# Filter rotation straight from float32, a cosine table made by a matmul, a fourth spectrum buffer and a new order table

## The chip, the cores and the metric

The kernel runs on one core of one Trainium2 chip. Its engines are TensorE (PE for matmuls, PEld for loading their stationary operands), VectorE (DVE), ScalarE (ACT), GpSimd (POOL) and SyncE (SP), which here issues every DMA. The metric is the device time of one execution in microseconds (us); less is better. Three runs of the kernel before gave 462.65, 462.97 and 460.04; their median is 462.65.

## What is computed

`x` and `f_logit` are 4 x 6272 x 256 (batch, time, channel), float32. The first half is a gated recurrence over time, the second a long convolution of its output, done in the frequency domain and gated on both sides:

```python
    f = lower_bound + (1 - lower_bound) * sigmoid(f_logit); i = 1 - f
    for t in range(S):                       # S = 6272
        h = f[:, t] * h + i[:, t] * x[:, t]; y[:, t] = h
    proj = y @ w_proj                        # 256 -> 3 * 256
    x1, x2, x3 = split(proj)
    conv = irfft(rfft(x2, axis=time) * rfft(filter_fft, axis=time))
    out = (x1 * conv * x3) @ w_out
```

## The kernel before

The length 6272 is 49 x 128, so each transform is done in two steps by matmuls with small tables of sines and cosines, kept in `D1`, `FT`, `VA`, `VB` and `ID` (in float16) and, for the filter, `D1r` and `FTr`. Work on one batch `b` goes through these steps, named as the planner names them:

- `hgrn(b)`: 13 chunks of 512 time steps. Each loads a piece of `f_logit` and of `x` (512 KB each, `load`, into three slots of `FL` and `XT`, for batch 0 also into `XS`), takes a sigmoid (`sig`, ScalarE, L334), a product (`u`, GpSimd, L336), and for each half of the channels transposes both (`su`, TensorE, L348), scales the gate (`f`, ScalarE L361 or VectorE L363) and runs the recurrence (`scan`, VectorE, L369) into `HA`. `wrap` copies the start of each sequence behind its end, on GpSimd, ScalarE or as a DMA of SP.
- `phase_p(b)` (`P`, L713) projects x2 and `x2` copies it into `X2`; `phase_f1`, `mini` and `unit` (`F1` L726, `F2` L785, `I2` L825) transform 16 units of 8 channel pairs forward and back. Between `F2` and `I2` each half unit is multiplied by the filter's spectrum: straight from PSUM on VectorE (L806), or copied by ScalarE or VectorE and multiplied on GpSimd (`pm`, L815). A unit's spectrum is loaded from DRAM into one of NH = 3 buffers `Hu` (`H`, L763); the order of use reverses from batch to batch, so that the buffers' contents serve twice at a turn.
- `gate(b)` (`x13`, L397, then `xs`, `z`) projects x1 and x3 and multiplies them into `zt`.
- `phase_o(b)`: 13 groups of four rows (the last has one). `I1` (L865) ends the back transform, `y` (VectorE, L871) applies the gate, `proj` (L883) multiplies by w_out, `o` copies out of PSUM, `store` sends 512 KB to `out`. Staging buffers are three `osb` tiles (`NO`) and, for groups 3 to 6, borrowed room in `PP` and in the `A` part of `HA`.

`prepare` runs once, ahead of and beside `hgrn(0)`. It makes an identity (`iden`), rounds it to float32r as `rot`, computes the arguments of all tables on VectorE (`args0` for 520 columns, `args1` for 512 more, which only `ID` needs), takes sines of both on ScalarE (L559) and fills the tables. It scales w_proj and copies w_out on ScalarE (seven `W` operations). The filter comes in 13 loads (`ff`) into ten buffers, seven in `X2`, two in `Hu`, one in `HA`. A group is first rounded to float32r by a copy (`fr`) into `afs`, then each of its rows is rotated by a matmul with a window of `rot` (`rot`, L629), which shifts its partitions; two copies (`f2`) bring it to the layout of the first filter step. When all thirteen groups are there, `FF1` (L654), `afs`, `FF2` (L672) and `hw` make the filter's spectrum and `hst` (L681) stores it to DRAM. Twenty-four fillers (`warm`, L599, four float16 matmuls each) may be put anywhere on TensorE.

The order is not that of the code. `Plan.op` records every operation with its reads, writes and engines; the string `ORDER` then lists, in the order in which they are emitted, each operation's number, engine and PSUM bank. Each engine runs its own in that order, and SP issues its DMAs in that order, so an operation that waits holds up what stands behind it on its engine. The planner that made the string is not part of the kernel.

## Time and profile before

| | us |
|---|---|
| median of three runs | 462.65 |
| profiled execution, its own time | 464.51 |
| its span in the profile | 462.3 |
| TensorE busy / idle in the span | 440.1 / 22.2 |
| first matmul of FF1 | 23.0 |
| first matmul of P, batch 0 | in 60 to 80 |

The page names an instruction by line, engine, operation, output and inputs, shape and count; then come busy time and mean duration, and the engine's idle time just ahead of it with what ended most of that. Views by time give start and length in us. Views by stage give busy time of each engine, the clock that TensorE was granted (1.00 is full) and the mean busy share of the core's 16 DMA engines. Rows of the page that the prediction does not use:

```profile
PEclk9799999999999999999999999999999899999999
DMA  8999999857987995668959983787969822655176
...
L336 POOL TENSOR_TENSOR XT<-XT,FL 128x1024 f32<-128x1024 f32 (+1 forms) x49 | 109.8, 2243 | 60.3 <-ACT FL L334 40.9
L369 DVE TENSOR_TENSOR_SCAN HA<-fTs,HA,PS 128x512 f16<-128x512 f32 (+1 forms) x96 | 112.5, 1202 | 6.3 <-ACT fTs L361 5.5
L815 POOL TENSOR_TENSOR PP<-HA,Hu 98x1008 f16<-98x1008 f16 x52 | 109.2, 2107 | 10.0 <-ACT HA L283 8.6
L397 PE MATMUL PS<-HA,W 128*128 128x490 f16 (+1 forms) x416 | 101.5, 367 | 0.8 <-DVE HA L369 0.5
```

The first two lines cut the span into 40 slices, in tenths: TensorE's granted clock and the DMA engines' busy share.

### The profile page before, as it was taken

To read this page: it belongs to the slowest core of one execution; us is meant where nothing else is said; L and a number is where in the kernel's file an instruction comes from. 1 tells how busy PE (TensorE), PEld (TensorE's weight loads), DVE (VectorE), ACT (ScalarE), POOL (GpSimd) and SP (SyncE) were. 2 spreads that over 40 slices of the span, in tenths; PEclk is the share of its full clock that TensorE was granted. 3 is DMA by queue.
4 is the path that set the end of the run, shared out by engine and by line. 5 is a ranking of instruction groups with operands and counts; after the bars stand their busy time and mean duration, and the time that the engine had idled before them with its cause. 6 is when DMAs were issued, how large, how long until landed. Compare 5 with 4: busy or idle time off the path is not lost.

```text
span 462.3 us, 14627 instructions
## 1 busy us (share of the span) xinstructions
PE 440.1 (95%) x6009; PEld 347.8 (75%) x6009; DVE 408.1 (88%) x475; ACT 403.6 (87%) x577; POOL 310.3 (67%) x283
## 2 busy tenths in 40 slices
PE   7799889999999999999999999999999899999998
PEld 5677668767767889777668898676768797767787
DVE  8889988799999994899999987999999847999963
ACT  5899898899999989999998988999999778988462
POOL 6978795476999634978997526889986303876400
PEclk9799999999999999999999999999999899999999
DMA  8999999857987995668959983787969822655176
GB/s 323 408 349 336 357 316 339 306 155 214 342 293 253 342 358 181 227 193 272 338 212 331 363 276 145 229 298 262 333 214 300 309 92 84 196 181 183 59 304 255
DMA packets 44530, 121.66 MB, mean 263 GB/s; under 512 B 4272, under 2 KB 6960, under 8 KB 44464
## 3 DMA queue, kind: packets, MB, share of 16 engines
q1 hardware_dynamic: 44464, 120.73, 74.8%
q8 instruction: 47, 0.77, 0.7%
q14 instruction: 19, 0.16, 0.1%
HBM read 87.69 MB, written 31.98 MB: 259 GB/s over the span
## 4 chain that ended last, share of the span: by engine, by line
PE 64%; DVE 11%; ACT 9%; DMA 6%; POOL 5%; issue 4%; SPq 1%; DVEq 0%; POOLq 0%; ACTq 0%
PE PS L397 16%; PE PS L825 8%; PE PS L883 7%; PE PS L713 7%; PE PS L348 7%; PE PS L785 6%; PE PS L726 6%; DVE HA L369 5%; DMA FL<-in_f_logit_dram 3%; PE PS L865 3%; DVE ys L871 3%; POOL XT L336 2%; POOL PP L815 2%; ACT FL L334 2%; ACT fTs L361 1%
## 5 line engine op out<-in xcount | busy, mean ns | idle before, releaser
L336 POOL TENSOR_TENSOR XT<-XT,FL 128x1024 f32<-128x1024 f32 (+1 forms) x49 | 109.8, 2243 | 60.3 <-ACT FL L334 40.9
L369 DVE TENSOR_TENSOR_SCAN HA<-fTs,HA,PS 128x512 f16<-128x512 f32 (+1 forms) x96 | 112.5, 1202 | 6.3 <-ACT fTs L361 5.5
L815 POOL TENSOR_TENSOR PP<-HA,Hu 98x1008 f16<-98x1008 f16 x52 | 109.2, 2107 | 10.0 <-ACT HA L283 8.6
L397 PE MATMUL PS<-HA,W 128*128 128x490 f16 (+1 forms) x416 | 101.5, 367 | 0.8 <-DVE HA L369 0.5
L806 DVE TENSOR_TENSOR PP<-PS,Hu 98x1008 f16<-98x1008 f32 x76 | 89.9, 1200 | 4.2 <-PE PS L785 2.0
L283 ACT CAST HA<-PS 128x1024 f16<-128x1024 f32 (+1 forms) x104 | 83.0, 828 | 3.4 <-PE PS L785 1.5
L871 DVE TENSOR_TENSOR ys<-PS,zt 128x1024 fp32r<-128x1024 f32 (+1 forms) x52 | 58.3, 1151 | 10.6 <-PE PS L865 7.8
L361 ACT ACTIVATE fTs<-PS,nomc 128x512 f32<-128x512 f32 (+1 forms) x93 | 60.3, 669 | 3.0 <-PE PS L348 2.0
L883 PE MATMUL PS<-Wo,ys 128*128 128x256 f32 x392 | 58.5, 296 | 1.2 <-DVE X L288 0.6
L825 PEld LDWEIGHTS <-PP 98*128 98x128 f16 x1024 | 49.5, 98 | 12.4 <-POOL PP L790 2.6
L397 PEld LDWEIGHTS <-W 128*128 128x128 f16 x416 | 35.1, 97 | 29.6 <-issue 5.0
L285 ACT ACTIVATE XS<-PS 128x490 f32<-128x490 f32 (+1 forms) x90 | 51.6, 585 | 6.5 <-PE PS L397 4.3
L283 ACT CAST Th<-PS 128x784 f16<-128x784 f32 x61 | 50.1, 822 | 5.8 <-PE PS L825 4.8
L883 PEld LDWEIGHTS PS<-Wo,ys 128*128 128x128 f32 x392 | 50.5, 192 | 6.2 <-DVE ys L871 1.3
L334 ACT ACTIVATE FL<-FL 128x1024 f32<-128x1024 f32 (+1 forms) x49 | 49.3, 1012 | 6.7 <-DMA FL<-in_f_logit_dram 6.6
L418 DVE TENSOR_TENSOR zt<-PS,XS 128x490 f16<-128x490 f32 (+1 forms) x81 | 51.3, 649 | 3.4 <-PE PS L397 2.1
L825 PE MATMUL PS<-VA,PP 98*128 98x98 f16 x512 | 52.4, 207 | 1.3 <-POOL PP L790 0.8
L825 PE MATMUL PS<-VB,PP 98*128 98x98 f16 x512 | 52.1, 207 | 0.0
L427 POOL TENSOR_TENSOR zt<-XS 128x490 f16<-128x490 f32 x23 | 28.3, 1234 | 28.5 <-DVE ys L871 21.7
L713 PE MATMUL PS<-W,HA 128*128 128x256 f16 x392 | 44.1, 273 | 1.2 <-ACT X L283 0.6
L348 PE MATMUL PS<-iden,FL 64*128 64x64 f32 x736 | 41.9, 230 | 3.0 <-ACT PP L285 1.5
L713 PEld LDWEIGHTS <-HA 128*128 128x128 f16 x392 | 42.9, 142 | 2.1 <-issue 1.6
(117 smaller groups left out, 728.7 us busy)
## 6 DMA issues: line engine op xcount, KB each, us to landing
Hu<-H SPq DMA_DIRECT2D x55, 512.0 KB, 4.4
FL<-in_f_logit_dram SPq DMA_DIRECT2D x45, 512.0 KB, 6.1
XT<-in_x_dram SPq DMA_DIRECT2D x45, 512.0 KB, 6.5
out_dram<-osb SPq DMA_DIRECT2D x32, 512.0 KB, 4.1
X<-in_moe_filter_fft_dram SPq DMA_DIRECT2D x9, 512.0 KB, 7.6
out_dram<-PP SPq DMA_DIRECT2D x8, 512.0 KB, 6.1
out_dram<-HA SPq DMA_DIRECT2D x8, 512.0 KB, 4.4
H<-Hu SPq DMA_DIRECT2D x4, 512.0 KB, 7.5
```

The lines of the kernel that those rows point to most:

```text
L283: nc.scalar.copy(dst, src)
L336: op("u", {"POOL": 0.1 + 0.553 * nb}, lambda e, xt=xt, ft=ft: nc.gpsimd.tensor_tensor(xt, xt, ft, op=AOP.mult), r=[("ft", k)], w=[("xt", k)])
L348: nc.tensor.transpose(bank(pb)[:, at[p] + j:at[p] + hn:nb], src[ps, j, cols], iden[ps, ps])
L361: nc.scalar.activation(fT, sT, AF.Identity, scale=by, bias=1.0)
L369: nc.vector.tensor_tensor_scan(h, fT, bank(pb)[:, 512 - hn:512 + hn], init, op0=AOP.mult, op1=AOP.add),
L397: nc.tensor.matmul(PS[:, p, 0:n], W13[:, kh, js], HA[:, HB[kh] + t0:HB[kh] + t0 + n], start=(kh == 0), stop=(kh == 1))
L713: nc.tensor.matmul(pp[:, r - r0, :], column(HB[kh], q_of(r)), W2[:, kh, :], start=(kh == 0), stop=(kh == 1))
L806: nc.vector.tensor_tensor(pr, px.unsqueeze(1).broadcast_to([TB, 2, UE, 63]), hh, op=AOP.mult)
L815: nc.gpsimd.tensor_tensor(pr, spec[:, o, :, 1:64].unsqueeze(1).broadcast_to([TB, 2, UE, 63]), hh, op=AOP.mult)
L825: nc.tensor.matmul(PS[:, ib + o, pr * TB:(pr + 1) * TB], PP[:TB, k, o, n, 2 * pr:2 * pr + 2, :], v[:TB], start=(n == 0), stop=(n == 1))
L871: nc.vector.tensor_tensor(late["ys"][:, yk, :, 0:rn * 128], PS[:, cb:cb + 2, 0:rn * 128], late["zt"][:].rearrange("p k r m -> p k (r m)") ...
L883: nc.tensor.matmul(po[:, i, :], late["ys"][:, yk, kh, i * 128:(i + 1) * 128], Wo[:, kh, :], start=(kh == 0), stop=(kh == 1))
```

## The change

- Filter groups 0, 2, 4, 6, 8 and 10 (`WHOLE`) are no longer rounded: their rows are rotated straight from the loaded float32 data, with the same identity read as plain float32 (`rot4`, 24 matmuls). The seven others keep the `fr` copy.
- The arguments shrink from 1032 columns to 324: of each table only the sine and the cosine remain, and the others are made from these by sign. `args1` is gone; the sign columns become one operation (`signs`), which the order puts on GpSimd. `ID` is now made on TensorE by four matmuls of the first table with the identity (`flip`) and one ScalarE activation that scales by `wt` and repeats it (`flipped`).
- The seven `W` operations may run on GpSimd, and the order puts all seven there.
- The fillers go from 24 to 14; 6 instead of 11 of them stand in the front, 3 in the middle instead of 1, 3 among the last groups of outputs instead of 1, and 2 behind the last projection instead of 11.
- A fourth spectrum buffer (`Hl`) is made once the filter's scratch room is free: `NH` = 4, of which `NK` = 3 are in `Hu`. There are 52 loads `H` instead of 55.
- Two own staging buffers instead of three; `places` says where each output group is staged (`PP` is used for groups 2, 3, 8 and 9, the `A` part for 4 and 5). A place in `zt` is programmed and not used.
- `ORDER` is replaced as a whole. Between engines, over the whole kernel, it moves little: of `wrap` 26 instead of 32 are on GpSimd, 7 instead of 8 on ScalarE and 15 instead of 8 on SP; of the copies `A` 11 instead of 7 are on VectorE, of `xs` 19 instead of 15; the direct products on VectorE are 77 instead of 76.

```diff
-NH = 3
-NO = 3
-WARM = 24
+NH = 4
+NK = 3
+NO = 2
+WARM = 14
+WHOLE = (0, 2, 4, 6, 8, 10)
...
-            op("W", {"ACT": 0.6}, lambda e, kh=kh, by=by: act.activation(
+            op("W", {"ACT": 0.6, "POOL": 0.75}, lambda e, kh=kh, by=by: scaled(
...
-        small(iotas, 1260, r=["iden"], w=st + ["pint", "FT"], e="POOL", kind="iota")
+        small(iotas, 452, r=["iden"], w=st + ["pint", "FT"], e="POOL", kind="iota")
...
-            for i, k in enumerate((kre, kre, k2, k2)):
+            for i, k in enumerate((kre, k2)):
                 stt(w[:, 128 + 98 * i:226 + 98 * i], in0=cF, scalar=k,
-                    in1=oF[i], op0=AOP.mult, op1=AOP.add)
-            fold(0, 520)
-
-        def args1(e):
+                    in1=oF, op0=AOP.mult, op1=AOP.add)
+            fold(0, 324)
+
+        def signs(e):
...
-        def rest2(e):
+        def flip(e, p):
             for i in range(2):
-                pool.tensor_scalar(ID[:, i, :], in0=v[:, 520 + 256 * i:776 + 256 * i],
-                                   scalar1=wt, scalar2=None, op0=AOP.mult)
+                for h in range(2):
+                    nc.tensor.matmul(PS[64 * h:64 * h + 64, p, i * 128:i * 128 + 128],
+                                     v[:, i * 64:i * 64 + 64], iden[:], start=True, stop=True)
+
+        def table(e, p):
+            act.activation(ID[:].rearrange("p i (c j) -> p i c j", c=2),
+                           PS[:, p, 0:256].rearrange("p (i j) -> p i j", i=2).unsqueeze(2)
+                           .broadcast_to([128, 2, 2, 128]), AF.Copy, scale=wt)
...
-            op("fr", {"ACT": 0.08 + 0.214 * rn, "POOL": 0.1 + 0.235 * rn, "DVE": 0.1 + 0.267 * rn},
-               lambda e, raw=raw, fr=fr, rn=rn: copy(e, fr[:, 0:rn], raw[:, 0:rn]),
-               r=et, w=[("af", g % 2, 0), ("af", g % 2, 1)])
-            def rotate(e, pb, r0=r0, rn=rn, fr=fr):
+            whole = g in WHOLE
+            if not whole:
+                op("fr", {"ACT": 0.08 + 0.214 * rn, "POOL": 0.1 + 0.235 * rn, "DVE": 0.1 + 0.267 * rn},
+                   lambda e, raw=raw, fr=fr, rn=rn: copy(e, fr[:, 0:rn], raw[:, 0:rn]),
+                   r=et, w=[("af", k, 0), ("af", k, 1)])
+
+            def rotate(e, pb, r0=r0, rn=rn, fr=raw if whole else fr, rot=rot[:].bitcast(F32) if whole else rot):
                 pr = PS[:, pb:pb + 2].rearrange("m a (r e) -> m (a r) e", e=256)
                 for r in range(r0, r0 + rn):
                     nc.tensor.matmul(pr[:, r - r0, :], rot[:, m0_of(r):m0_of(r) + 128],
                                      fr[:, r - r0, :], start=True, stop=True)
-            rt = op("rot", {"PE": 0.12 * rn}, rotate, r=[("af", g % 2, 0), "rot"], take=2)
+            rt = op("rot4" if whole else "rot", {"PE": (0.43 if whole else 0.12) * rn}, rotate,
+                    r=(et if whole else [("af", k, 0)]) + ["rot"], take=2)
...
+    def hu(h):
+
+        return Hu[:, h] if h < NK else late["Hu"][:]
...
+    places = (("o", 0), ("o", 1), ("p", 0), ("p", 1), ("a", 0), ("a", 1), ("o", 0),
+                  ("o", 1), ("p", 0), ("p", 1), ("o", 0), ("o", 1), ("o", 0))
```

302 lines of the change are left out of this document (161 added, 141 removed).

## The prediction

> **What bounds the kernel now.** I read the page first (busy times, chain), then the busy time by stages, then the front (0 to 23 us) in order of time, then the stage behind it, and last the seams between batches and the tail.
>
> ```profile
> PE 440.1 (95%) x6009; PEld 347.8 (75%) x6009; DVE 408.1 (88%) x475; ACT 403.6 (87%) x577; POOL 310.3 (67%) x283
> ...
> PE 64%; DVE 11%; ACT 9%; DMA 6%; POOL 5%; issue 4%; SPq 1%; DVEq 0%; POOLq 0%; ACTq 0%
> ```
>
> TensorE is busy 440.1 of 462.3 us and carries 64% of the chain that ended last, so a saving on another engine counts only where it shortens TensorE's 22.2 us of idle time, or work that TensorE alone does. Where that idle time lies, the stages tell (start:end, length, then busy time of PE, PEld, DVE, ACT, POOL, granted clock, DMA share, GB/s):
>
> ```profile
> 0.00:23.00 23.00, 17.52 (x93) 13.63 (x94) 19.62 (x49) 16.42 (x26) 18.48 (x37) 0.85 0.94 365
> 23.00:60.00 37.00, 32.81 (x429) 26.17 (x430) 34.49 (x38) 34.47 (x50) 29.82 (x30) 1.00 0.98 350
> 60.00:100.00 40.00, 38.56 (x440) 30.46 (x437) 34.02 (x39) 35.77 (x52) 26.39 (x29) 1.00 0.82 280
> 100.00:300.00 200.00, 195.27 (x2878) 154.19 (x2875) 183.98 (x200) 186.62 (x266) 146.07 (x115) 1.00 0.78 267
> 300.00:400.00 100.00, 95.68 (x1408) 76.39 (x1408) 86.89 (x95) 90.51 (x133) 63.05 (x51) 0.98 0.69 236
> ```
>
> TensorE idles 5.5 us in the front, 4.2 in the next stage, 1.4 up to 100 us, then 4.7 in 200 and 4.3 in the next 100. The front is paced by DMA (share 0.94), and from 23 to 60 us VectorE and ScalarE are both 93% full (34.5 of 37): that stage, filter transform with the first recurrence, belongs to them.
>
> **The front: six casts out, 24 plain float32 matmuls in.** In order of time (start, length):
>
> ```profile
> 8.68 1.86 SPq L618 DMA_DIRECT2D X<-in_moe_filter_fft_dram  x3
> ...
> 23.00 2.92 PE L654 MATMUL PS<-D1r,f 128*128 128x256 f32 x20 [0.48 <-ACT f L283]
> ```
> ```profile
> X<-in_moe_filter_fft_dram SPq DMA_DIRECT2D x1, 128.0 KB, 9.3
> ```
> ```profile
> 1.64 5.95 DMA X<-in_moe_filter_fft_dram
> ...
> 8.67 1.28 ACT L559
> ...
> 12.27 0.60 PE PS L599 x4
> 12.87 0.63 PE PS L629 x4
> ...
> 20.19 1.23 PE PS L629 x4
> 21.45 1.73 ACT f L283 x4
> ```
>
> The third of the thirteen filter loads lands at 7.59 (1.64 + 5.95); the last is issued at about 10.2, as the end of three issues that finish at 10.54, and lands 9.3 later, at 19.5. Between the two lie 9.25 groups in 11.9 us: 1.28 each, so the second lands at 6.3 and the twelfth at 19.1. Behind the last come its rotation and evacuations; ScalarE's queue of evacuations ends at 23.18, and FF1 starts at 23.0. A group's four rotations take 0.63 at one time and 1.23 at another, which the granted clock explains (columns as above):
>
> ```profile
> 12.00:14.00 2.00, 1.21 (x8) 0.82 (x7) 2.00 (x2) 2.00 (x5) 1.94 (x2) 1.00 1.02 408
> 14.00:22.00 8.00, 7.33 (x30) 6.08 (x31) 6.55 (x11) 6.73 (x13) 7.60 (x12) 0.57 1.03 408
> ```
>
> A mean of 0.57 over 8 us, if the clock knows only full and half, is half for 6.9 of them; it fell after a stretch in which TensorE was busy 1.21 of 2 us.
>
> The change leaves the loads, so nothing before 19.5 can be won. What it does to the 3.5 us behind: the sine table load (1.28, at 8.67) leaves the middle of ScalarE's work, because the sine is now ScalarE's first instruction and its table loads while nothing has landed; two of its twenty evacuations go to VectorE, which no longer computes a second block of arguments. On TensorE a group straight from float32 costs an unknown; no plain float32 matmul of 256 columns is in the trace. Bounds by the nearest rows: below, the rounded rotation, 0.63 for four; above, the 512-column matmul of FF2:
>
> ```profile
> L672 PE MATMUL PS<-afs,FTr 64*128 64x512 f32 x64 | 11.0, 437 | 0.3 <-ACT afs L283 0.2
> ```
>
> 437 ns each, 1.75 for four. The nearest row in columns is the lower one, but its operands are the rounded ones that these groups give up; I take 1.75, since a lower price would win little more. Then six such groups and seven others (the last has one matmul) are 6 x 1.75 + 6 x 0.63 + 0.2 = 14.5 us, from the second landing on to 20.8. TensorE is nearly full, so that its clock should stay up, and it ends with the twelfth group (group 8): landed at 19.1, rotated by 20.9, the single matmul by 21.1, evacuated by 21.6. FF1 starts at about 21.7: 1.3 earlier. At 0.63 it would be 20.6, 2.4 earlier.
>
> The Trainium skill, FP8 and Floating Point Precision, section TensorE Precision Notes, says that true float32 makes four passes through the array; by that a group would cost an estimated 4 x 0.63 = 2.5, which I keep as a rival.
>
> New waits: the load of group 10 waits for the rotation of group 0, and that of group 12 for group 2's, the sixth on TensorE, ending at 6.3 + 4 x 1.75 + 2 x 0.63 = 14.6; on SP's queue behind it stand all loads of batch 0. The twelve groups ahead keep the DMA engines busy to 19.1, and a load takes some 4 us on an empty queue (the third's 5.95 less the 1.28 of each of two ahead, 3.4, is the nearest), so SP has about 1 us in hand: 0, but late from then on.
>
> The front's fillers go from 11 (four matmuls each, 0.60) to 6; nine of the eleven ran before the first rotation, so they cost and save nothing but the clock.
>
> **23 to 72 us.** The order tables say which engine does what between the last evacuation and the last scan of batch 0. ScalarE: seven W operations leave, copies of `afs` go from 18 to 22, of `hw` from 11 to 13, `f` from 19 to 17, one table activation enters. VectorE: `afs` 14 to 10, `hw` 3 to 2, `f` 7 to 9.
>
> ```profile
> L361 ACT ACTIVATE fTs<-PS,nomc 128x512 f32<-128x512 f32 x7 | 4.6, 686 | 0.4 <-PE PS L348 0.2
> L283 ACT CAST afs<-PS 128x512 fp32r<-128x512 f32 x8 | 4.6, 585 | 0.3 <-issue 0.3
> L285 ACT ACTIVATE Hu<-PS 128x1024 f16<-128x1024 f32 x4 | 4.1, 1016 | 0.0
> ...
> L476 ACT ACTIVATE W<-HA,omc 128x512 f16<-128x512 f32 x2 | 1.4, 750 | 0.0
> L481 ACT ACTIVATE W<-HA,omc 128x128 f16<-128x128 f32 x3 | 1.3, 438 | 0.0
> ```
> ```profile
> L288 DVE CAST afs<-PS 128x512 fp32r<-128x512 f32 x14 | 9.1, 678 | 1.0 <-issue 0.6 <-PE PS L672 0.4
> ```
>
> ScalarE: -2 x 0.75 - 4 x 0.44 for six W operations, about -0.6 for the seventh, +4 x 0.59, +2 x 1.02, -2 x 0.69, and some 0.7 for the table, a copy of 512 elements: about 0. VectorE: -4 x 0.68 = -2.7; its one spectrum copy less and two `f` more cancel, at ScalarE's prices to 0.4: -2.3. So the pair is 2.3 lighter, with one spectrum copy more done inside the stage, and the stage starts 1.3 earlier.
>
> GpSimd pays: it takes the seven W operations and the sign columns, and loses five casts, the ID table and two wraps.
>
> ```profile
> L589 POOL TENSOR_SCALAR ID<-PP,cols 128x256 f16<-128x256 f32 x2 | 1.8, 927 | 0.0
> ...
> L576 POOL TENSOR_SCALAR FT<-PP,cols 128x98 f16<-128x98 f32 x2 | 1.1, 576 | 0.0
> ```
>
> From 98 to 256 elements a scaling grows from 576 to 927 ns, 2.2 ns an element: 1.5 for each W13 half, 0.64 for each W2 piece, and by the same line 1.5 at most for Wo, a copy: 7.1 us at most, put around the third and fourth products of batch 0, with the recurrence behind them. The ID table (1.8) is gone, and the memset of X2's gaps, inside this stage before, now stands ahead of it: at most 5.3 net. GpSimd has 7.2 us of idle in 23 to 60, so this fits, if just; of TensorE's 4.2 idle there I count 1.5 as won (bounds: 2.5 won, 2.5 lost when GpSimd is late).
>
> **Seams and the rest.** The matmul work of the batches is the same, and switches between full and half-row work on TensorE are 208 before and 206 after, so no price. The largest seam stall, before batch 3:
>
> ```profile
> 353.67 8.79 DMA FL<-in_f_logit_dram
> ```
> ```profile
> 363.00:366.00 3.00, 1.38 (x40) 1.12 (x36) 1.85 (x2) 3.00 (x5) 2.36 (x1) 1.00 0.68 263
> 366.00:370.00 4.00, 3.97 (x37) 3.85 (x38) 4.00 (x4) 2.51 (x5) 0.74 (x1) 0.57 0.74 286
> ```
>
> A load lands 8.8 us after issue, because it stands behind two stores; ScalarE's evacuation stands behind the sigmoid of that load; TensorE idles 1.6 in 363 to 366, and then its clock is at 0.57 for 4 us, worth 1.7. In the new order loads 20 to 23 of batch 3 are issued ahead of store 1, so this landing comes two transfers earlier. I count 2.0 of the 3.3 as won; the rest I leave to new stalls of the same kind.
>
> Here the clock fell after 1.38 busy of 3 us, in the front after 1.21 of 2. The Trainium skill, TensorE: Matmul & The Clock Gate, section on HAM oscillation, asks for an idle gap above about 3.4 us; this trace disagrees: there was no room for one in either stretch.
>
> Fourth H buffer: 55 loads become 52; none of the sixty longest waits names a landed spectrum, so 0 either way. Seven more wraps go by SP: 7 x 0.6 less on GpSimd, not the bound there, 0. Output staging with two own buffers: the last group shares one with the group two before it, and four projections or fillers lie between, longer than a store's landing: 0. Fillers behind the front: before two ahead of the last projection, after six, 0.6 each; up to 2.4 if none is covered by a wait, I take 0.8 lost. The tail:
>
> ```profile
> 455.58 4.82 PE PS L599 x44
> ```
> ```profile
> 450.01 8.00 SPq L894 DMA_DIRECT2D out_dram<-osb  x6
> ```
> ```profile
> SPq L961 <- DMA out_dram<-osb: 3.1, 1, 3.1
> ```
>
> Eleven fillers run behind the last projection to 460.4, but SP, whose last store is issued by 458.0, waits 3.1 more for its landing, to 461.1: their removal saves nothing.
>
> **Sum.** The profiled run took 464.51 (span 462.3 and 2.2 around it). -1.3 - 1.5 - 2.0 + 0.8 = -4.0: 460.5. It stands 1.9 above the median 462.65; the same change from the median is 458.7. I take half a microsecond off the gain for stalls that a wholly new order opens: **459.2**.
>
> **Rivals.** (1) TensorE waits less everywhere: the 4.2 of the second stage go wholly and a third of the 10.4 behind it; 459.2 - 2.7 - (3.5 - 2.0) = 455.0. For it: VectorE lighter, a buffer more. Against: ScalarE no lighter there. (2) Idle time only moves: the front's gain is swallowed at the seams, as both copying engines stay full; 462. (3) GpSimd becomes the bound of the second stage: its 7.1 us of scalings delay the fourth product by 4.0 (less the 1.3 of the earlier start and the 1.8 taken away), of which the bound above lets 2.5 reach TensorE, instead of winning 1.5; 459.2 + 4.0 = 463.2. (4) Slower: the front becomes TensorE's. It decides if four float32 rotations take over 1.8, for then 6.3 + 6x + 4.0 is later than 19.1 + x + 0.2. At four times the rounded row, 2.5, rotation ends at 25.3 instead of 21.1: 463.4. If the clock falls as before as well, 6.9 us at half lose 3.4 more: 466.8. For it: TensorE has no slack at 1.75 already; against: a full TensorE is what kept the clock up in every other window. By the passes on the page named above and this row its first half would be certain. (5) Slower: the new order keeps the stall at 363 and makes another two like it: 459.2 + 2.0 + 6.6 = 467.8. (6) That the change does not do what it says: the sine's table could still load late; ScalarE's order excludes it, no chance.
>
> **Chances.** Forecast (457 to 462) 0.35; (1) 0.16; (2) 0.17; (3) 0.11; (4) 0.14; (5) 0.07. One per cent of 462.65, about what a measurement here can tell from no change, is 4.6: faster is under 458.0, slower over 467.3. Faster: (1) and 0.14 of the forecast, 0.30. Slower: 0.05 of (5) and 0.04 of (4), 0.09. Same: 0.61. The range goes from 454.5, under (1), to 466, near (4)'s end, and leaves out (5) and the rims.
>
> **What would show it.** Right: FF1's first matmul near 21.7; four float32 rotations near 1.75; clock 1.00 through 6 to 22; TensorE's idle in the second stage under 3; no wait over 1 us at the seam of batch 3. Wrong: rotations still running after 23, GpSimd without gaps from 24 to 50 with TensorE waiting on transposes, the clock at 0.5 in the front, or more than 11 us of TensorE idle behind 60.

## The result, and the profile after

The changed kernel took **458.62 us**, the median of 9 runs (456.89 to 460.24), beside 462.97 for the kernel before on the same chip (9 runs, 460.04 to 465.8): a ratio of 0.9922, 95% interval 0.9893 to 0.9951. The forecast was 459.2. A second set, run later, gave 457.84 beside 461.23, ratio 0.9925 (0.9902 to 0.9948). Its profiled run took 459.04, with a span of 457.2, where that of the kernel before had taken 464.51 and 462.3. The counts of runs and of clocks below leave out executions that were disturbed as a whole, three of e_nh3's six among them.

So the time came out as forecast; how it came about did not, in several steps. Busy times and the first line of the chain on the page of the changed kernel:

```profile
PE 438.0 (96%) x6001; PEld 347.9 (76%) x6001; DVE 402.7 (88%) x458; ACT 397.0 (87%) x564; POOL 304.7 (67%) x285
...
PE 67%; DVE 9%; ACT 9%; issue 6%; POOL 5%; DMA 3%; POOLq 0%; DVEq 0%; ACTq 0%; SPq 0%
```

TensorE has 2.1 us less work and 3 us less idle time (19.2 of 457.2, before 22.2 of 462.3). By stages (columns as in the prediction: start:end, length, busy time of PE, PEld, DVE, ACT, POOL, granted clock, DMA share, GB/s):

```profile
0.00:23.00 23.00, 20.05 (x105) 16.33 (x105) 12.18 (x30) 12.47 (x20) 16.91 (x46) 1.00 0.93 357
23.00:60.00 37.00, 34.05 (x440) 27.36 (x440) 33.45 (x37) 35.87 (x50) 33.71 (x34) 1.00 0.96 347
60.00:100.00 40.00, 38.04 (x446) 30.39 (x446) 33.65 (x38) 36.69 (x53) 18.75 (x20) 1.00 0.91 323
...
300.00:400.00 100.00, 98.23 (x1440) 77.99 (x1439) 92.60 (x103) 89.54 (x131) 68.17 (x57) 1.00 0.68 233
```

The clock stands at 1.00 where it was 0.85 and 0.98. TensorE's idle time in the second stage goes from 4.2 to 3.0 and in 300 to 400 from 4.3 to 1.8. But ScalarE and VectorE, 4.0 and 7.4 us lighter in the front than before, did not bring FF1 forward. The front's end, in order of time (start, length, engine, line, operation, and in brackets the idle time before it and what ended it):

```profile
17.72 1.89 PE L645 MATMUL PS<-X,rot 128*128 128x256 f32 x8
...
19.26 0.82 PE L645 MATMUL PS<-afs,rot 128*128 128x256 f32 x4
...
19.92 1.89 PE L645 MATMUL PS<-Hu,rot 128*128 128x256 f32 x8
...
21.56 0.37 PE L645 MATMUL PS<-afs,rot 128*128 128x256 f32 x1
21.86 0.66 PE L594 MATMUL PS<-iden,PP 128*64 128x128 f32 x8
...
21.92 0.69 DVE L294 CAST f<-PS 128x512 fp32r<-128x512 f32 x1 [0.51 <-PE PS L645]
...
22.64 0.91 ACT L289 CAST f<-PS 128x512 fp32r<-128x512 f32 x2 [1.25 <-DVE f L294]
...
23.61 2.58 PE L672 MATMUL PS<-D1r,f 128*128 128x256 f32 x17 [1.09 <-ACT f L289]
```

Group 10 is rotated from 17.72, the last full group, 8, from 19.92 to about 21.5; VectorE copies its second half, and ScalarE's copy of the first half, the one that FF1 reads, begins 0.03 after VectorE's has ended. FF1's first matmul runs at 23.61, where it ran at 23.00 before.

The table shows where the profiled runs, those of the experiments too, stand at the points that matter (us from the span's start; each row is one profiled run, the median and the ratio are those of its timed runs). The old and the new order end differently, so the ends of the last projection compare only between rows of the same order.

| kernel | FF1 starts | P of batch 0 starts | from I1 of batch 2 to P of batch 3 | last projection ends | span | median | ratio to before (95%) |
|---|---|---|---|---|---|---|---|
| before | 23.00 | 74.3 | 30.3 | 455.6 | 462.3 | 462.97 | |
| after | 23.61 | 71.9 | 27.6 | 453.2 | 457.2 | 458.62 | 0.9922 (0.9893 to 0.9951) |
| after, again | 22.93 | 72.0 | 27.6 | 452.7 | 456.7 | 457.84 | 0.9925 (0.9902 to 0.9948) |
| e_evac | 22.57 | 71.3 | 27.7 | 452.0 | 455.5 | 457.68 | 0.9930 (0.9903 to 0.9958) |
| e_g8r_evac | 22.25 | 71.3 | 27.7 | 451.9 | 455.6 | 457.35 | 0.9950 (0.9924 to 0.9976) |
| e_front | 21.89 | 71.2 | 27.6 | 451.9 | 457.7 | 457.47 | 0.9934 (0.9908 to 0.9960) |
| e_wact | 22.85 | 72.9 | 27.7 | 453.6 | 457.6 | 459.88 | 0.9982 (0.9951 to 1.0012) |
| e_fill | 23.30 | 71.6 | 27.6 | 451.9 | 456.3 | 459.77 | 0.9971 (0.9950 to 0.9992) |
| e_nofill | 22.00 | 70.8 | 27.6 | 452.6 | 456.1 | 457.47 | 0.9928 (0.9901 to 0.9955) |
| e_round | 27.71 | 76.2 | 27.6 | 456.8 | 461.3 | 463.85 | 1.0074 (1.0042 to 1.0106) |
| e_nh3 | 22.84 | 71.4 | 27.6 | 468.5 | 473.2 | 474.53 | 1.0225 (1.0134 to 1.0316) |
| before: e_seam | 21.81 | 71.3 | 27.6 | 449.9 | 456.2 | 459.73 | 0.9965 (0.9931 to 0.9998) |
| before: e_straight | 23.33 | 75.0 | 28.6 | 457.5 | 463.2 | 461.53 | 1.0002 (0.9967 to 1.0037) |
| before: e_clock | 21.66 | 74.8 | 27.6 | 453.6 | 459.9 | 460.78 | 0.9976 (0.9941 to 1.0010) |

One column is missing there because it belongs to whole sets: the granted clock. In 93 runs of the kernel before, from four later sets, the mean clock was under 0.998 in 50, down to 0.982; the median of those 50 is 461.56, that of the other 43 is 460.33. In 21 runs of the changed kernel it was never under 0.998.

### The profile page after: what moved, and what is told of

Its sections match the earlier page's. It is cut to its first block, busy times and chain, and to the rows that moved or that the text cites. A ratio compares the mean times of both kernels' runs of the same rounds, so it can differ in the third digit from the quotient of the medians.

```text
span 457.2 us, 14624 instructions
## 1 busy us (share of the span) xinstructions
PE 438.0 (96%) x6001; PEld 347.9 (76%) x6001; DVE 402.7 (88%) x458; ACT 397.0 (87%) x564; POOL 304.7 (67%) x285
## 4 chain that ended last, share of the span: by engine, by line
PE 67%; DVE 9%; ACT 9%; issue 6%; POOL 5%; DMA 3%; POOLq 0%; DVEq 0%; ACTq 0%; SPq 0%
PE PS L403 15%; PE PS L930 10%; PE PS L354 8%; PE PS L849 7%; PE PS L731 7%; PE PS L807 6%; PE PS L744 5%; DVE HA L375 4%; PE PS L912 3%; PE PS L645 2%; ACT HA L289 2%; PE PS L610 2%; DMA FL<-in_f_logit_dram 2%; POOL XT L342 2%; DMA XT<-in_x_dram 1%
## 5 line engine op out<-in xcount | busy, mean ns | idle before, releaser
L403 PE MATMUL PS<-HA,W 128*128 128x490 f16 (+1 forms) x416 | 99.8, 367 | 0.7 <-ACT XS L291 0.3
L839 POOL TENSOR_TENSOR PP<-HA,Hu 98x1008 f16<-98x1008 f16 x40 | 84.1, 2109 | 7.4 <-ACT HA L289 7.2
L289 ACT CAST HA<-PS 128x1024 f16<-128x1024 f32 (+1 forms) x102 | 80.2, 816 | 5.6 <-PE PS L744 2.8
L830 DVE TENSOR_TENSOR PP<-PS,Hu 98x1008 f16<-98x1008 f32 x56 | 66.0, 1197 | 1.4 <-PE PS L849 0.7
L403 PEld LDWEIGHTS <-W 128*128 128x128 f16 x416 | 35.7, 97 | 30.4 <-issue 3.8
L289 ACT CAST Th<-PS 128x784 f16<-128x784 f32 x63 | 51.2, 822 | 4.1 <-PE PS L849 3.6
L433 POOL TENSOR_TENSOR zt<-XS 128x490 f16<-128x490 f32 (+1 forms) x23 | 28.0, 1223 | 39.2 <-DVE ys L918 20.6
```

The costliest lines, as they stand in the source:

```text
L289: nc.scalar.copy(dst, src)
L403: nc.tensor.matmul(PS[:, p, 0:n], W13[:, kh, js], HA[:, HB[kh] + t0:HB[kh] + t0 + n], start=(kh == 0), stop=(kh == 1))
L830: nc.vector.tensor_tensor(pr, px.unsqueeze(1).broadcast_to([TB, 2, UE, 63]), hh(), op=AOP.mult)
L839: nc.gpsimd.tensor_tensor(pr, spec[:, o, :, 1:64].unsqueeze(1).broadcast_to([TB, 2, UE, 63]), hh(), op=AOP.mult)
```

## The experiments

The order of the work is a coded table in the kernel; its edits are shown decoded, an operation and its engine a line.

**The last evacuations (e_evac).**

```diff
 rotation, group 8          TensorE
-copy group 8, 2nd half     VectorE
-copy group 8, 1st half     ScalarE
+copy group 8, 1st half     ScalarE
 rotation, group 12         TensorE
-copy group 12, 1st half    ScalarE
-copy group 12, 2nd half    VectorE
+copy group 12, 1st half    VectorE
+copy group 8, 2nd half     VectorE
+copy group 12, 2nd half    ScalarE
```

> The changed kernel, with the evacuations of the last two filter groups dealt out anew: the first half of group 8 (the half that the first FF1 reads) goes first, on ScalarE, the first half of group 12 goes to VectorE, the two second halves follow. Theory: in the changed kernel FF1 started at 23.61 because ScalarE's copy of group 8 stood behind VectorE's copy of the same two banks (21.92 to 22.61), with group 12's behind it; then FF1's first matmul comes at 22.7 here, 0.9 earlier, and the time falls by 0.5 to 0.9 against the 458.6 of the changed kernel. Rival 1: the copies are not in each other's way and the rotation's end at 21.92 is what counts; FF1 stays within 0.2 of 23.6. Rival 2: FF1 starts at 22.7, but the stage behind it is VectorE's and ScalarE's and swallows it; the third product of batch 0 starts at 71.9 as before and the time stays at 458.6.

Measured: the same stretch of its profile, in order of time:

```profile
21.85 0.93 ACT L288 CAST f<-PS 128x512 fp32r<-128x512 f32 x2 [0.46 <-PE PS L644]
...
21.97 0.39 DVE L293 CAST f<-PS 128x128 fp32r<-128x128 f32 x1 [0.56 <-PE PS L644]
...
22.55 0.69 DVE L293 CAST f<-PS 128x512 fp32r<-128x512 f32 x1 [0.19 <-ACT f L288]
22.57 2.69 PE L671 MATMUL PS<-D1r,f 128*128 128x256 f32 x18
```

FF1 comes at 22.57 with the rotations at the same times as in the first profile of the changed kernel, so 1.04 earlier: the theory's place and size. Now VectorE waits for ScalarE instead: in neither kernel do the two copy out of these banks at once. P of batch 0 starts 0.6 to 0.7 earlier (71.3), and the last projection ends 0.7 to 1.2 earlier; the median, 457.68, lies under both medians of the changed kernel, but the intervals of the ratios overlap.

Fronts are best compared from a point that all share, since whole fronts shift by up to 0.7 from one execution to the next. From the start of group 10's rotation to FF1 it takes 5.89 in both profiles of the changed kernel (23.61 less 17.72, 22.93 less 17.04) and 4.84 here.

**One group less straight from float32 (e_g8r_evac).**

```diff
-WHOLE = (0, 2, 4, 6, 8, 10)
+WHOLE = (0, 2, 4, 6, 10)
 cast group 11              VectorE
+cast group 8               VectorE
```

besides the edit of e_evac.

> As the run with the evacuations dealt out anew, and besides group 8, the last full group to land, is rounded on VectorE and rotated as a rounded group again (five groups straight from float32 instead of six). Theory: the float32 rotation of this group, 1.54 from start to start with TensorE behind (it began 1.26 after the landing), costs more than the cast of 0.68 and a rotation of 0.8: rotation of the last group ends at 21.0 instead of 21.9, and FF1 starts at 22.1, bound by ScalarE's queue of copies. Rival: VectorE's cast pushes back its copies of group 11, and nothing is won against the same kernel without the cast: 22.7. Time: 0.9 to 1.5 under the changed kernel's 458.6 by the theory, 0 to 0.9 by the rival.

Measured: FF1 at 22.25, but the whole front runs 0.25 ahead; from group 10's rotation it is 4.77, 0.07 less than in e_evac. The rival is right: the cast on VectorE and the wait for it cost what the float32 rotation of this group did. P of batch 0 stays at 71.3. The time, 457.35, lies in the theory's band, but that is no sign for it: e_evac without this cast had 457.68, and the intervals overlap.

**All that could be moved in the front (e_front).**

```diff
-rotation and copies of group 12   bank 0
+rotation and copies of group 12   bank 2
 FF1, first three
+turning of the cosines, and its copy
```

besides the edits of e_g8r_evac, with the turning of the cosines taken from ahead of the first FF1 and group 11's first half copied ahead of its second.

> As the run with group 8 rounded and the evacuations dealt out anew (FF1 at 22.25, with TensorE waiting 0.57 for a bank ahead of group 12's rotation and the turning of the cosines, 0.65, just ahead of FF1), with group 12's rotation in a bank that is free earlier, the turning of the cosines behind the third FF1, and group 11's first half copied first. Theory: FF1 starts at 21.7 to 21.9, when ScalarE's copy of group 8 ends, and the time falls by 0.3 to 0.5 against that kernel, 1.3 to 1.8 under the changed one. Rival: the stage behind the front is bound by ScalarE and VectorE from its first operation on, and the turned cosines' copy now stands among them; P of batch 0 starts at 71.3 as in that kernel, and the time is the same.

Measured: FF1 at 21.89, 4.27 behind group 10's rotation, as the theory had it, and P at 71.2, as the rival had it. Against the first profile of the changed kernel FF1 is 1.7 earlier, the first scan 1.3 (29.1 and 30.4), the ninth 1.0 (45.1 and 46.1), P 0.7. The gain leaks away step by step in a stage in which VectorE and ScalarE are over nine tenths full; no new wait of TensorE marks the place, and which step takes it was not separated.

**The seam of batch 3 alone (e_seam), in the kernel before.**

```diff
+load f_logit, chunk 11, batch 3
+load x, chunk 11, batch 3
 store 1, batch 2
 store 2, batch 2
-load x, chunk 11, batch 3
-load f_logit, chunk 11, batch 3
```

> The kernel before, with one thing of the new order: the two loads of the twelfth chunk of batch 3 are issued ahead of the second and third store of batch 2, the gate's load first. Theory: the stall of 1.6 us and the half clock of 3.4 us at 363 to 370 hang on this landing alone; both go, P of batch 3 starts at 369.6 to 370.0 instead of 372.3 and the time falls from 463.0 to 460.4. Rival 1: the changed kernel's gain here comes from the rest of its order (the share of ScalarE and VectorE in the evacuations); the loads alone give under 0.7. Rival 2: the stores now land later and hold up a staging buffer or the next stage; P starts earlier but the time stays within 0.5 of 463.0.

Measured: from I1 of batch 2 to the first product of batch 3 it takes 27.6 instead of 30.3, to a tenth what the changed kernel takes, and the stretch that had the stall is full (columns as above):

```profile
363.00:366.00 3.00, 2.31 (x36) 1.99 (x36) 2.92 (x4) 2.21 (x5) 0.70 (x1) 1.00 0.61 240
366.00:370.00 4.00, 4.00 (x56) 3.90 (x50) 3.86 (x4) 2.31 (x4) 0.00 (x0) 1.00 0.57 224
```

The place is the theory's. The time fell by 0.35% (0.02 to 0.69), 1.6 us, with the 2.6 expected inside the interval of 0.1 to 3.2. The surprise stands in the front of this run, which nobody had touched:

```profile
12.00:14.00 2.00, 1.32 (x8) 0.81 (x7) 2.00 (x3) 2.00 (x5) 2.00 (x2) 1.00 1.03 410
14.00:22.00 8.00, 5.68 (x34) 4.40 (x35) 6.39 (x11) 7.30 (x15) 8.00 (x14) 1.00 1.03 406
```

The clock stays at 1.00 where the profiled run of the kernel before had 0.57 in 14 to 22, with 1.32 of 2 us busy ahead of it instead of 1.21; FF1 starts at 21.81 instead of 23.00. So the fall in the front is not a property of the kernel but of some of its executions: in 7 of 12 runs of e_seam the mean clock is under 0.998.

**The weights back on ScalarE (e_wact).**

```diff
-W, seven operations   GpSimd
+W, seven operations   ScalarE
```

> The changed kernel with the seven operations on the weights back on ScalarE, at the same places of the order. Theory: of the 3.0 us that the stretch from FF1 to the first product gained, the larger part comes from GpSimd's taking these 4.2 us of ScalarE's work; then P of batch 0 starts 1.5 to 3.0 later than 71.9 and the time is 460.1 to 461.6. Rival: ScalarE has that much in hand and the gain comes from the other deal of evacuations and from the order; P of batch 0 starts under 0.7 later, and the time is within 0.7 of 458.6. Second rival: GpSimd, 91% busy from 23 to 60 us, was the bound, and the time falls.

Measured: with FF1 at nearly the same time as in the second profile of the changed kernel (22.85 and 22.93), P of batch 0 starts at 72.9 instead of 72.0: 0.9 later, between the theory's 1.5 and the rival's 0.7. This is kept to the end (453.6 and 452.7). The busy times of 23 to 60 show the change of hands, ScalarE at 99% and GpSimd 7 us lighter than in the changed kernel:

```profile
23.00:60.00 37.00, 33.27 (x424) 26.48 (x424) 32.54 (x36) 36.59 (x54) 26.64 (x26) 1.00 0.96 342
```

The medians are further apart, 459.88 and 457.84, and the intervals of the ratios just miss each other. GpSimd at 34 of 37 us was not the bound.

**The yardstick (after_again).**

> The changed kernel once more, unaltered, as the yardstick for the runs beside it. By its first runs: 458.6, FF1 at 23.6, the first product of batch 0 at 71.9, clock 0.998 or more in every run.

Measured: 457.84, FF1 at 22.93, P of batch 0 at 72.0, no clock under 0.998. FF1 differs by 0.7 between two executions of one kernel, P by 0.1.

**All groups rounded (e_round).**

```diff
-WHOLE = (0, 2, 4, 6, 8, 10)
+WHOLE = ()
 loads, rotations and copies of the front: in the order of the kernel before
+cast, groups 1, 2, 5, 7, 9, 10, 11, 12   VectorE
+cast, groups 3, 4, 6, 8                  GpSimd
+cast, group 0                            ScalarE
```

> The changed kernel with all thirteen filter groups rounded first, none rotated straight from float32: loads, rotations and evacuations of the front in the order of the kernel before, the casts dealt to VectorE (8), GpSimd (4) and ScalarE (1); six fillers, the early sine and everything behind the front as in the changed kernel. The kernel before with two loads moved had, in one execution without a fall of the clock, FF1 at 21.8; the profiled kernel before, with its clock at half for 6.8 us, had it at 23.0. Theory: the rounded rotations leave TensorE half idle, and the clock falls in the front of some executions, so that the mean granted clock is below 0.998 in a third of the runs or more, and FF1 comes between 21.5 and 23.0; the straight rotations bought a steady clock, not an earlier FF1. Rival: the steady clock comes from fewer waits (the sine's table and second block of arguments gone), and the clock stays at 0.998 or more in nearly all runs; then FF1 comes at 21.5 to 22.0 and the time falls by 1 to 2 against the changed kernel.

Measured: worse than either, FF1 at 27.71. The waits of TensorE in its front, in order of time:

```profile
14.38 1.23 PE L644 MATMUL PS<-afs,rot 128*128 128x256 f32 x4 [1.72 <-POOL afs L300]
...
17.76 2.05 PE L644 MATMUL PS<-afs,rot 128*128 128x256 f32 x8 [2.15 <-DVE afs L293]
...
21.66 2.04 PE L644 MATMUL PS<-afs,rot 128*128 128x256 f32 x8 [1.86 <-DVE afs L293]
```
```profile
0.00:23.00 23.00, 13.31 (x62) 10.14 (x63) 11.29 (x29) 9.60 (x16) 14.64 (x38) 0.81 0.93 358
```

Each rotation waits for a cast, each cast for the rotation two back that frees its buffer, and dealt to three queues they wait for one another. The row by itself is the busy time by stage: TensorE works 13.3 of 23 us and the clock is 0.81; in all nine runs it is 0.985 or less. The theory's clock is right, its FF1 is 4.7 off at the near end, because of this deal of the casts; what a better deal would reach isn't shown. Nor does it show what the straight rotations by themselves do for the clock, since this deal makes TensorE wait besides. Useful beside it: against the first profile of the changed kernel, 4.1 us later at FF1 are 4.2 at P and 4.1 at the end. A front that is 4 us late costs in full here, while one that is 1.7 early (e_front) pays in part, and the 0.7 between the two profiles of the changed kernel are 0.1 at P.

**The fillers (e_fill, e_nofill).** Six behind the front moved behind the last projection:

```diff
-filler at 261, 267, 308, 448.6, 451.2, 452.0
 last projection
+six fillers
 two fillers
```

> The changed kernel with the six fillers behind the front (at 261, 267, 308, 448.6, 451.2 and 452.0) put behind the last projection. By the prediction's term they cost 0.8: the time falls by 0.8, and by 2.4 at most, the last phase (first I1 of batch 3 to the end of the last projection, 23.4) shrinks by 0.3 to 1.2. Rival: each stands in a wait for an evacuation or a product of VectorE that lasts as long without it; the time stays within 0.3 of the changed kernel's. Second rival: without them the clock falls in some runs, and the time rises.

Measured: by the profile the rival is right. From the first I1 of batch 3 to the issue of the last store it takes 23.81 (428.6 to 452.41) against 23.96 in the second profile of the changed kernel: each filler stood in a wait. But the median is 459.77, 1.9 above the changed kernel's, though the profiled run, with 458.09 the fastest of the twelve, shows nothing of it. The second rival's falls are there, in 4 of 12 runs (mean clock 0.993 to 0.996), but they don't explain the 1.9: the median of the other eight, all at 1.000, is 459.5. The next run took the fillers out, all eight:

```diff
-WARM = 14
+WARM = 6
```

with the edit of e_evac.

> The changed kernel with the evacuations of the last two filter groups dealt out anew (the run that had 457.7) and all eight fillers behind the front taken out, the two at the end too. The run with six of them put to the end (eight there, 3.7 us) had its last store landed as early as the changed kernel by its profile, and still a median 1.9 above it. Theory: the time behind the last projection is a race between the landing of the last stores (issue to landing 1.8 to 4.9 us so far) and TensorE's fillers, and these run on at half clock where the clock falls there; without them only the landing counts: the median comes to 456.3 to 457.3, and falls of the clock behind the last projection cost nothing. Rival 1: the fillers at 261, 267 and 308 us hold up the clock; without them it falls there, the mean clock is under 0.998 in a third of the runs, and the median stays above 458.5. Rival 2: neither; 457.4 to 458.0, as the kernel with the fillers.

Measured: 457.47, 0.2 under the same kernel with its fillers, just over the theory's band and inside the second rival's. The mean clock is under 0.998 in 10 of 12 runs, far more than the third that the first rival named, though its median above 458.5 didn't come. In the profiled run (0.996) that is one fall at the very end. Two windows of its end (columns as above):

```profile
449.00:452.60 3.60, 1.89 (x14) 1.42 (x14) 1.04 (x2) 1.40 (x2) 0.00 (x0) 1.00 0.74 291
452.60:456.00 3.40, 0.00 (x1) 0.00 (x0) 0.42 (x1) 0.00 (x0) 0.00 (x0) 0.50 0.51 195
```

TensorE is busy 1.89 of 3.6 us around the last projection, and the clock halves as it ends. Here nothing is left to run at half speed, so this fall costs nothing. It can take the mean down to 0.996 at most; three runs are lower (0.991 to 0.995) and so have another fall, whose place isn't known. In e_fill eight fillers stand there, 3.67 us at full clock and twice that at half, which would be past the landing of the last store (455.4 in its profile). But the record speaks against this as the cause of its 1.9: eight of its twelve runs show no fall and are as slow. The cause stays open.

**Straight rotations alone (e_straight), and fillers in their place (e_clock), in the kernel before.**

```diff
+WHOLE = (0, 2, 4, 6, 8, 10)
-cast, groups 0, 2, 4, 6, 8, 10
-rotation of these groups, rounded
+rotation of these groups, float32
```

> The kernel before with one part of the change alone: the six even filter groups are rotated straight from float32 and their six casts are gone (one on ScalarE, four on GpSimd, one on VectorE); order, tables and engines otherwise as before. In the runs of the kernel before so far the mean granted clock was under 0.998 in about half, in the changed kernel's 21 runs in none. Theory: the float32 rotations, at 1.54 each in place of 0.63, fill TensorE's waits in the front, so that the clock stays up there: the clock is under 0.998 only where the seam before batch 3 still stalls (0.996, one fall of 3.4 us), never under 0.995, and FF1 comes at 22.5 to 23.2, P of batch 0 at 71.5 to 73; time 459.5 to 461, 0 to 1.5 under the kernel before. Rival: the clock was kept by the changed kernel's other waits (no second sine, fewer fillers), and falls here as often as before, to 0.989 and below. Second rival: TensorE becomes the front's bound in this order too, FF1 comes later than 23.6 and the time rises by 0.5 or more.

```diff
-WARM = 24
+WARM = 33
 the edit of e_seam
+filler of two matmuls ahead of the rotations of groups 2 to 9 and 11
```

> The kernel before with the two loads of batch 3 ahead of the two stores (as in the run on that seam) and, besides, nine half fillers (two matmuls each, 0.3 us) ahead of the third to eleventh rotation in the front, all groups rounded. Without the fillers that kernel had a clock under 0.998 in 7 of 12 runs and a median of 459.7; in the one execution profiled, where it did not fall, FF1 came at 21.8. Theory: what the change bought in the front is the clock alone, and fillers in the waits buy it as well, without float32 rotations: clock 0.998 or more in at least 10 of 12 runs, FF1 at 21.7 to 22.3, and a median of 457.5 to 458.5, level with the changed kernel or better. Rival: the fillers delay the rotations as much as they save (each stands ahead of one), FF1 comes after 23 and the median stays above 459.5. Second rival: half fillers are too little, the clock falls as often as without.

Measured: both profiled runs keep the clock up in the front, and in no run of either is the mean under 0.996, which is one fall of 3.4 us; 7 of 12 and 5 of 12 have it, so e_clock misses the 10 of 12 without a fall that its theory asked for. In both profiled runs the one fall comes later, in the second stage, behind a stretch in which TensorE was little over half busy. First e_straight, then e_clock:

```profile
0.00:23.00 23.00, 21.26 (x117) 17.50 (x117) 16.15 (x48) 14.98 (x24) 15.73 (x35) 1.00 0.94 367
...
57.00:61.00 4.00, 2.25 (x41) 1.74 (x40) 3.09 (x4) 4.00 (x6) 3.71 (x5) 1.00 1.02 415
61.00:64.40 3.40, 3.23 (x27) 2.60 (x28) 3.13 (x4) 3.11 (x5) 2.72 (x3) 0.50 0.96 350
```
```profile
55.00:59.00 4.00, 2.22 (x38) 1.40 (x36) 3.96 (x5) 2.90 (x4) 3.44 (x6) 0.99 0.96 367
59.00:62.40 3.40, 3.40 (x38) 3.11 (x34) 2.22 (x4) 2.78 (x4) 1.87 (x2) 0.50 0.89 340
```

TensorE's wait at that place, in the kernel before, in e_clock, in e_seam and in the changed kernel (waiter, what it waited for, sum, times, longest):

```profile
PE PS L348 <- ACT PP L285: 1.5, 1, 1.5
```
```profile
PE PS L347 <- ACT PP L284: 1.8, 1, 1.8
```
```profile
PE PS L346 <- ACT PP L283: 0.5, 1, 0.5
```
```profile
PE PS L354 <- DVE HA L375: 0.4, 1, 0.4
```

In the old order a transpose waits for ScalarE's copies of two spectra, which stand behind the sigmoid of a load. How long ScalarE waits for that load differs from execution to execution: 0.95 us in the kernel before, 1.25 in e_clock, 1.17 in e_straight, nothing in e_seam. In the profile of the new order this wait is gone. e_straight's ratio is 1.0002: the part of the change that its name begins with buys nothing that shows by itself. FF1 came at 23.33, 0.1 outside the theory's range, P at 75.0, far outside it. e_clock had FF1 at 21.66 and P still at 74.8: its theory is wrong where it says that the front's clock was what the change bought.

**Three buffers of H (e_nh3).**

```diff
-NH = 4
+NH = 3
+load of H: one more in each of batches 1 to 3, others later where the buffer is taken
```

> The changed kernel with three buffers of H instead of four: 55 loads of H instead of 52, each as late in the order as the third buffer back allows. By the prediction the fourth buffer is worth 0: the time is within 0.5 of the changed kernel's 457.8 to 458.6, and TensorE's idle time between 100 and 400 us, 6.3 there, stays under 7.3. Rival: with the new deal of products to GpSimd the buffers come free later and the spectra land late: TensorE waits on products whose H is still loading, and the time rises by 1 to 4.

Measured: far past the rival, 2.25% slower than the kernel before (1.34 to 3.16). Two lines of its waits, of a kind that the changed kernel doesn't have:

```profile
DVE PP L829 <- DMA Hu<-H: 8.8, 5, 3.4
...
POOL PP L838 <- DMA Hu<-H: 7.6, 4, 3.7
```

VectorE and GpSimd wait 16.4 us for spectra, and between 100 and 400 us TensorE idles 15.5 instead of 6.3. The order was made for four buffers; what three would cost in an order made for three is another question, and the kernel before had three and no such wait among its longest.

## Why the prediction was right, point by point

**The front: -1.3 forecast, +0.6 and -0.1 in two profiles.** Here the prediction failed, but not by its price for a float32 rotation. One matmul compares as follows (shortest, median, longest ns of a record; straight, then rounded), and two rounded groups in a row as the third line shows:

```profile
L645 PE MATMUL PS<-X,rot x40: 378/379/634, 6.4 to 19.2; 128*128 128x256 f32 x40
L645 PE MATMUL PS<-afs,rot x25: 276/281/469, 10.1 to 21.6; 128*128 128x256 f32 x25
...
15.49 1.19 PE L645 MATMUL PS<-afs,rot 128*128 128x256 f32 x8 [0.64 <-ACT f L289]
```

A record lasts longer than the step to the next one, because matmuls overlap, so a price has to be taken from the steps. A straight matmul is two records whose starts lie 0.216 us apart at full clock, 1.73 for four; a rounded one is a single record, 0.12 apart, 0.48 for four. The sum's 1.75 was right, by luck: the row that it came from, FF2's, runs two matmuls at a time. Its 0.63 for a rounded group was too dear, since it has the last record's run-out in it. A straight and a rounded group together take 2.20 (17.72 to 19.92) where the sum had 2.38. The 1.54 of the expectations, from start to start, is too low, because the rounded group behind starts its first matmul beside the last straight one.

The Trainium skill, FP8 and Floating Point Precision, section TensorE Precision Notes, which stood beside rival 4, gives true float32 four passes; this trace nearly agrees, with 0.43 for a straight matmul, 3.6 times the 0.12 of a rounded one. Four times 0.63 came out too high because of the run-out.

The clock, too, was as forecast, 1.00 from 7.2 us on. The step that failed is "it ends with the twelfth group: landed at 19.1, rotated by 20.9, the single matmul by 21.1, evacuated by 21.6". The group landed at 18.66, but TensorE was 1.26 behind and had waited another 1.1 on banks and casts; the six fillers, at half clock, held the first rotation back to 6.44, where the sum let it start at 6.3, and it ran at half clock itself until 7.2; and from the last rotation to FF1 it took 1.7 instead of 0.6, because two copies from one pair of banks went one after the other, with the half that FF1 needs second. e_evac turned the two round and won 1.04 of it. The Trainium skill, PSUM — Partial Sum Buffer, section PSUM bank collisions raise a hardware error, says that the compiler back end adds a dependency between instructions of two engines that touch the same bank in the same 32 partitions, reads included; the trace agrees, with 0.03 between the end of one copy and the start of the other in either order.

And the step compared with the wrong run. 23.0 was the FF1 of an execution in which the clock had fallen; without a fall the old front reaches it at 21.8 (e_seam) or, with fillers, 21.7 (e_clock). Against that the new front is 1 to 2 us late.

**The second stage: -1.5 forecast, -2.3 to -3.0 measured** (FF1 to P 51.3 before, 48.3 and 49.0 after). Reason and place hold: GpSimd's load fits, TensorE's idle time is 2.95 and 2.39, under the 3 named as a sign. e_wact shows 0.9 of it to be the weights' change of hands. But 51.3 is one execution too: e_seam, whose order differs only from 350 us on, took 49.5 (21.81 to 71.33), without the wait for a late load. Against that the new order wins 0.5 to 1.2, less than forecast, and the rest of the 2.3 to 3.0 is a stall that the old order has in some executions. In four profiles of the old order the stage took 49.5 to 53.2, in nine of the new one 48.3 to 49.3 (50.1 in e_wact), so the new order is the steadier one. That this comes from having no transpose behind those copies is argued.

**The seam: -2.0 forecast, -2.7 measured,** and e_seam shows that the place of two loads does it alone. Here as well part is chance: e_straight, with the loads at the old place, took 28.6 with no fall of the clock there, so 1.0 of the 2.7 was won against that execution and 1.8 more against the profiled one. The mechanism was right; what was left for "new stalls of the same kind" wasn't needed.

**Fillers behind the front: +0.8 forecast, 0.15 measured** by e_fill's profile. They stand in waits. The other part of that step, "eleven fillers run behind the last projection ... their removal saves nothing", holds for the profiled run. e_fill's median of 1.9 more, gone in e_nofill, is not explained: falls of the clock can't be the main reason (the eight runs without one have 459.5), and its profile shows nothing of it.

**The tail: 0 forecast, 0 measured** as a sum: from the first I1 of batch 3 to the end 27.6 before and 27.4 after. It is made up otherwise, though: the new order holds the one-row group back, takes 2.5 longer to the last projection and 2.7 less from there to the end.

**Fourth buffer: 0 forecast; not so in this order.** "None of the sixty longest waits names a landed spectrum" was true of the old order and says nothing of the new one, which issues products and loads otherwise; taken out of an order made for four, e_nh3, it costs far more than the whole change brings. What it is worth against the best order for three is not shown.

**The sum.** -1.3 - 1.5 - 2.0 + 0.8 = -4.0 came near because errors met, and that is luck. Between the first two profiles the span fell by 5.1: +0.6 in the front, -3.0 in the second stage, -2.7 at the seam, and 0.0 over the rest, where 1.4 was lost between P and I1 of batch 0, which no term had, and as much won in small pieces from there on. The second stage and the seam gave 2.2 more than forecast, the front 1.9 less, and the 0.8 for fillers wasn't lost. Rival 4, the front becomes TensorE's, holds in small part: its condition, over 1.8 for four, isn't met, and FF1 came at most 0.6 later than before, where its sum made that 2.9. What the front lost the stage behind made up.

Much of the 5.1 was won from stalls and falls of that one execution. e_seam, the old order with two loads moved, has a span of 456.2 in its profile, where the clock didn't fall, level with the 457.2 and 456.7 of the changed kernel, and its five runs without a fall have a median of 458.9, beside 458.62 and 457.84 for the changed kernel.

What the forecast didn't have is the clock as a matter of chance. The half of the executions of the kernel before that have falls, one to five by their mean clocks, are 1.2 us longer (461.56 against 460.33). In the profiles of the old order the clock fell at three places, the front, 59 to 64 us and the seam, and each goes with another part of the change: the float32 rotations, the new order of the second stage, and the two loads. This rests on one profile or two for each place. Mending the front alone (e_straight) or front and seam (e_clock) leaves falls; in the changed kernel the mean is never under 0.998. The Trainium skill, TensorE: Matmul & The Clock Gate, section What's actually happening, says that the clock is set by a free-running window of 3413 ns; the falls recorded here last 3.413, 6.827 or 13.653 us, and one program falls in one execution and not in the next, which agrees.

No version was shown to beat the changed kernel: e_evac, e_g8r_evac, e_front and e_nofill end the last projection 0.1 to 1.3 earlier and have medians of 457.35 to 457.68, under its 457.84 and 458.62, but within the intervals.

## What to carry to other kernels

Before a stall or a slow clock in one profile is priced, ask whether it is there in every execution: the granted clock of each timed run tells it, and here half of the runs didn't have what the profile showed. Ahead of a stage that two engines fill, an earlier front may pay only in part (here 0.7 of 1.7 us at P), and the cheapest gain was an order of copies: look for the operand that the next stage needs first, and let its copy go first. Take the price of a matmul from the steps between the starts of its records, not from their length. And a buffer that no wait names in the old order can be what a new order stands on.

## What the hardware showed that was not expected

The clock fell in mid-kernel with no gap of TensorE above 1.8 us. In the 3.4 us up to the fall TensorE was busy 1.84 us (before, from 11.19), 1.77 (before, from 362.75), 1.76 (e_straight, from 57.56) and 1.64 (e_clock, from 55.53). It did not fall behind 1.94 of 3.4 (before, from 55.6), 1.84 (e_straight, from 160.0) or 1.80 (e_seam, from 259.4). So these falls come where TensorE is busy about half of the time, but the busy time in the trace doesn't separate them cleanly, and one order lies on either side from execution to execution.

The landing of the last full store is a lottery. e_g8r_evac and e_front end their last projection at 451.9 both, and SP then waits for the stores (sum, times, longest), first e_g8r_evac, then e_front:

```profile
SPq L1009 <- DMA out_dram<-osb: 1.0, 2, 0.6
```
```profile
SPq L1009 <- DMA out_dram<-osb: 3.1, 2, 2.8
```

From issue to landing the same store took 2.6 and 4.9 us, and the spans are 455.6 and 457.7. That is more than any edit of the front won, so the end of a single span is no measure of one; the last projection's end is the better one.
